# Local V of batches 4 to 7 loaded by casting DMAs on GpSimd's queue, in a fused attention and MoE kernel

## The chip, the cores and the metric

One core of a Trainium2 chip runs the whole program. The metric is device time in microseconds (us). The engines are TensorE (PE, matrix products), VectorE (DVE), ScalarE (ACT), GpSimd (POOL) and SyncE (SP), which here only issues DMAs. Each engine runs its own list of instructions in order and waits on semaphores for the others. DMAs issued by SP and by GpSimd go to two queues, which share the core's 16 DMA engines.

## The reference

Eight batches, eight heads, 576 positions, head size 64. Heads 0 to 3 attend locally (the last 32 positions), heads 4 to 7 with a stride (all earlier positions of the same residue modulo 32). The result goes through a two-layer MLP with squared ReLU.

```python
mask_local = (rel >= 0) & (rel < stride)                      # stride = 32, heads 0..3
mask_strided = (rel >= 0) & (pos[None, :] % stride == pos[:, None] % stride)   # heads 4..7
scores = np.where(masks[None], 1/sqrt(D) * q @ k.T, -1e9)
attn = softmax(scores)
x = (attn @ v).transpose(0, 2, 1, 3).reshape(B * S, H * D)    # 4608 x 512
h = x @ w_in                                                  # 512 x 2048
return np.maximum(h, 0.0) ** 2 @ w_out                        # 2048 x 512, float32 out
```

All inputs are float32 in memory; the kernel computes in bfloat16 with float32 sums.

## The kernel before

**Units.** A unit is a pair of heads of one batch: `u = 4 * b + p`, with p = 0, 1 local and p = 2, 3 strided. For a unit the kernel transposes q and k (`step_T` on TensorE, or DMA transposes on SP in later batches), forms the scores (`step_S`, L315), takes the exponential (L320), masks, and multiplies by V (`step_D`, L419). The softmax sum comes out of the same product, because V has a column of ones (`VP` = 72 columns are kept for 65). `step_E` or `step_X` writes the transposed result into `xt`, from which `mm1` (L487) and `mm2` (L527) compute the MLP in nine chunks of 512 rows.

**Local V.** A local block has 96 queries and 128 keys: the 32 positions before the block and the block itself. So a tile of local V, `vls[i]`, holds for each of six blocks the block's own 96 rows in partitions 32 to 127, and in partitions 0 to 31 a copy of the last 32 rows of the block before. There are four such tiles; batch b uses tiles `(2 * b + p) % 4`, so a tile is used again after two batches.

**Three ways in which local V arrives.** Batch 0 has a load of its own (`load_v_first`, L353, and the shift L359). Batches 1 to 3 go through `loads` and use `load_v_local_cast` (L214), one DMA on GpSimd's queue that reads float32 and writes bfloat16 straight into partitions 32 to 127, and `shift_v_local` (L221), a GpSimd copy of partitions 96 to 127 to partitions 0 to 31 one block further on. Batches 4 to 7 go through `loads_v`: two DMAs per unit on SP's queue (`load_v_local`, L185) bring float32 rows into one of two staging tiles `vl_st`, and two GpSimd casts (`cast_v_local`, L192 and L193) write the tile and its shifted part. Partitions 0 to 31 of the staging tiles are zeroed once by VectorE at the start (L693).

**Strided V** of batches 2 to 7 is loaded on SP's queue into `v_st` (L201) and cast by GpSimd (L208), before and after the change.

**Order.** The program is written out by hand: `manual_schedule`. The MLP's groups are laid in a row, and attention steps are dealt out between them by weights (`due`). Loads hang on numbers of groups (`hooks`, set by `plan`). For batches from 4 on, `plan` places three things:

```python
        at(g, lambda: loads_qk(b))
        at(max(g + 8, g0 + (g1 - g0) * 8 // 10), lambda: transpose_str(b))
        at(n0, lambda: loads_v(b))
        for i in range(2):
            at(g + 14 + 4 * i, lambda u=4 * b + i: transpose_local(u))
```

A hook fixes only the order on each engine's list. GpSimd and SP run ahead of TensorE as far as their waits let them. On GpSimd the list of late batches repeats: the V work of batch b, then the DMAs that cast strided q and k of batch b + 1 to DRAM (`q_d`, `k_d`, L153), then four casts of local q and k of batch b + 1 (L123). On SP it is: the loads of local V, of strided V, loads of q and k (L107), transposes of `q_d` and `k_d` (L161), transposes of local q and k (L173), and between them the output (L532) and the transposes of finished attention (L444).

Of the kernel before, what the change touches and what calls it, by code (L numbers as in the profile page):

```python
# [8 lines left out]
FP32 = mybir.dt.float32  # L9
# [5 lines left out]
def kernel(  # L15
# [9 lines left out]
    nc = tc.nc  # L25
    B, H, S, D = q.shape
# [5 lines left out]
    QL = 96  # L32
    NL = S // QL
# [6 lines left out]
    singles = ctx.enter_context(tc.tile_pool(name="singles", bufs=1))  # L40
# [23 lines left out]
    mask_str = singles.tile([SP_, 1, SP_], BF16)  # L64
    vls = [singles.tile([128, 2, NL, VP], BF16, name=f"vl{i}") for i in range(NV)]
    vss = [singles.tile([SP_, NBS, VP], BF16, name=f"vs{i}") for i in range(NV)]
    vl_sts = [singles.tile([128, 2 * NL, D], FP32, name=f"vl_st{i}") for i in range(2)]
    kTl = [singles.tile([128, 32 + S], BF16, name=f"kTl{i}") for i in range(NV)]
    es = [singles.tile([128, 1280], BF16, name=f"e{i}") for i in range(4)]
    xt = [singles.tile([128, T], BF16, name=f"xt{p}") for p in range(4)]  # L70
# [21 lines left out]
    units = [(b, p) for b in range(B) for p in range(H // 2)]  # L92
    st = {}
# [83 lines left out]
    def v_slot(u):  # L177
        b, p = units[u]
        return (b * 2 + p % 2) % NV

    def load_v_local(u, eng):
        b, p = units[u]
        t = vl_sts[p]
        for hh in range(2):
            eng.dma_start(out=t[32:128, NL * hh:NL * (hh + 1), :],  # L185
                          in_=v[b, 2 * p + hh].rearrange("(t p) d -> p t d", p=QL))
        st.setdefault(u, {})["vf"] = t

    def cast_v_local(u):
        s = st[u]  # L190
        t = vls[v_slot(u)]
        nc.gpsimd.tensor_copy(t[:, :, :, 0:D].rearrange("p h t d -> p (h t) d"), s["vf"])  # L192
        nc.gpsimd.tensor_copy(  # L193
            t[0:32, :, 1:NL, 0:D],
            s["vf"][96:128].rearrange("p (h t) d -> p h t d", h=2)[:, :, 0:NL - 1, :])
        s["v"] = t

    def load_v_str(u, eng):
        b, p = units[u]
        t = v_st.tile([SP_, 2, NJ * D], FP32, name="v_st")  # L200
        eng.dma_start(out=t, in_=v[b, 2 * p:2 * p + 2]  # L201
                      .rearrange("h (p j) d -> p h (j d)", j=NJ))
        st.setdefault(u, {})["vf"] = t

    def cast_v_str(u, copy=None):
        s = st[u]
        t = vss[v_slot(u)]
        (copy or nc.gpsimd.tensor_copy)(t[:, :, 0:D], s["vf"].rearrange("p h (j d) -> p (h j) d", d=D))  # L208
        s["v"] = t

    def load_v_local_cast(u):
        b, p = units[u]
        t = vls[v_slot(u)]
        nc.gpsimd.dma_start(  # L214
            out=t.rearrange("p h t c -> p (h t) c")[32:128, :, 0:D],
            in_=v[b, 2 * p:2 * p + 2].rearrange("h (t p) d -> p (h t) d", p=QL))
        st.setdefault(u, {})["v"] = t

    def shift_v_local(u):
        t = vls[v_slot(u)]  # L220
        nc.gpsimd.tensor_copy(t[0:32, :, 1:NL, 0:D], t[96:128, :, 0:NL - 1, 0:D])  # L221
# [449 lines left out]

    def loads_v(b):
        for i in range(2):
            load_v_local(4 * b + i, nc.sync)
        for i in range(2):
            load_v_str(4 * b + 2 + i, nc.sync)
        for i in range(2):
            cast_v_local(4 * b + i)
        for i in range(2):
            cast_v_str(4 * b + 2 + i)  # L680

# [7 lines left out]
    warm(8)  # L689
    nc.vector.memset(ones, 1.0)  # L690
    nc.vector.memset(vl0[0:32, 0, 0, 0], 0.0)
    for t in vl_sts:
        nc.vector.memset(t[0:32], 0.0)  # L693
    for t in kTl:
        nc.vector.memset(t[:, 0:32], 0.0)
    for t in vls:
# [80 lines left out]
    def plan(b, n0, g0, g1):  # L777
        if b < LB:
            at(n0, lambda: loads(b))
            if b >= XB:  # L780
                at(n0 + 6, lambda: transpose_str(b))
            return
        g = g0 + (g1 - g0) * 45 // 100
# [5 lines that stand above are left out]
# [54 lines left out]
```

## Time and profile before

| | |
|---|---|
| median of 4 runs | 312.52 us (310.47 to 316.08) |
| the profiled execution | 313.4 us; span from first to last instruction 311.7 us |
| granted TensorE clock, mean | 0.989 |
| TensorE busy | 297.9 us (96%) |
| VectorE, ScalarE, GpSimd busy | 166.4, 162.6, 88.8 us |
| DMA, SP's queue | 72528 packets, 32.98 MB, 50.4% of 16 engines |
| DMA, GpSimd's queue | 19552 packets, 10.98 MB, 26.2% of 16 engines |
| loads of `vl_st` on SP | 16, first at 98.1, last at 180.7 us |
| casts L192 and L193 | 8 and 8, 0.959 us for one of the first kind in the mean |

How to read it: busy time is the sum of an engine's instructions. A row of a group gives line, engine, operation, the tile written and read, and then times; `x8: 823/824/1901` are count, and shortest, middle and longest duration in ns. In a list of windows, each engine's busy time in the window is followed by the number of its instructions, and after TensorE, its weight loads, VectorE, ScalarE and GpSimd come the granted clock, the share of the DMA engines and GB/s. In the timeline, square brackets hold the idle time before an instruction and what ended it.

### The profile page before, as it was taken

How to read it: one execution, taken by the hardware profiler on the slowest of the kernel's cores; microseconds unless marked ns; L12 is line 12 of the kernel's file. 1: busy time of each engine (PE TensorE's matmuls, PEld its weight loads, DVE VectorE, ACT ScalarE, POOL GpSimd, SP SyncE). 2: the span in 40 equal slices, each digit the busy share in tenths (PEclk: the TensorE clock that was granted, in tenths of full speed). 3: DMA queues.
4: the chain of work that ended last, by engine and by line, in shares of the span. 5: the costliest groups of instructions: out<-in, count | busy, mean ns of one | idle time of the engine just before them, and what ended most of it. 6: DMA issues, size and time to landing. Idle time of an engine off the chain costs nothing.

```text
span 311.7 us, 6150 instructions
## 1 busy us (share of the span) xinstructions
PE 297.9 (96%) x2326; PEld 149.5 (48%) x2368; DVE 166.4 (53%) x411; ACT 162.6 (52%) x338; POOL 88.8 (28%) x117
## 2 busy tenths in 40 slices
PE   7879997899999999999999999999999999999995
PEld 3534554545554544545444544444444444444444
DVE  7666666359866886577467667654522222222200
ACT  3937754388555765555555555655443434344311
POOL 8528864454720823381055024000000000000000
PEclk9979999799999999999999999999999999999999
DMA  7999999999999999999999792225122010000021
GB/s 141 160 206 211 208 193 252 205 271 187 207 133 216 209 212 169 205 243 214 175 215 202 164 201 80 73 72 55 53 74 86 34 37 34 34 34 36 36 98 67
DMA packets 92252, 44.40 MB, mean 142 GB/s; under 512 B 76544, under 2 KB 85536, under 8 KB 92032
## 3 DMA queue, kind: packets, MB, share of 16 engines
q1 hardware_dynamic: 72528, 32.98, 50.4%
q0 software_dynamic: 19552, 10.98, 26.2%
q8 instruction: 18, 0.29, 0.4%
q14 instruction: 10, 0.08, 0.1%
q10 hardware_dynamic: 144, 0.07, 0.1%
HBM read 36.70 MB, written 13.57 MB: 161 GB/s over the span
## 4 chain that ended last, share of the span: by engine, by line
PE 80%; DMA 13%; POOL 4%; issue 1%; DVE 0%; ACT 0%; DVEq 0%; POOLq 0%; ACTq 0%
PE ph L487 36%; PE py L527 26%; PE ph L527 9%; DMA vs<-in_v_dram 5%; DMA w_in_b<-in_moe_w_in_dram 4%; PE pt L419 4%; DMA w_out_b<-in_moe_w_out_dram 4%; PE pt L315 3%; PE pt L451 1%; PE pt L271 1%; POOL kT_s L133 1%; POOL qT_s L133 1%; PE pt L512 1%; PE ph L512 1%; POOL vs L227 1%
## 5 line engine op out<-in xcount | busy, mean ns | idle before, releaser
L487 PE MATMUL ph<-xt,w_in_b 128*128 128x512 bf16 x559 | 142.9, 381 | 1.3 <-issue 0.5
L493 ACT ACTIVATE r<-ph 128x512 bf16<-128x512 f32 x143 | 85.3, 597 | 95.6 <-PE ph L487 88.8
L494 DVE TENSOR_TENSOR g_sb<-r 128x512 bf16<-128x512 bf16 x144 | 72.4, 507 | 102.8 <-ACT r L493 102.0
L527 PE MATMUL py<-w_out_b,g_sb 128*128 128x512 bf16 x378 | 99.6, 379 | 1.1 <-DVE x_l L434 0.2
L487 PEld LDWEIGHTS <-w_in_b 128*128 128x128 bf16 x576 | 52.6, 98 | 57.5 <-issue 1.9
L527 PEld LDWEIGHTS <-g_sb 128*128 128x128 bf16 x560 | 51.0, 98 | 53.8 <-issue 0.6
L320 ACT ACTIVATE e<-pt 128x288 bf16<-128x288 f32 (+1 forms) x128 | 46.3, 407 | 12.8 <-PE pt L315 12.8
L527 PE MATMUL ph<-w_out_b,g_sb 128*128 128x512 bf16 x155 | 39.4, 386 | 0.5 <-issue 0.3
L419 PEld LDWEIGHTS <-e 128*128 128x128 bf16 (+1 forms) x392 | 20.9, 98 | 17.6 <-issue 2.9
L434 DVE TENSOR_TENSOR x_s<-pt,rinv 72x384 bf16<-72x384 f32 (+1 forms) x42 | 21.4, 509 | 1.4
L192 POOL CAST vl<-vl_st 128x768 bf16<-128x768 f32 x8 | 7.7, 959 | 49.6 <-DMA vl_st<-in_v_dram 24.8
L326 DVE TENSOR_TENSOR e<-e,mask_loc 128x576 bf16<-128x576 bf16 x32 | 16.3, 511 | 3.7 <-ACT e L320 3.7
L531 ACT COPY y<-py 128x512 f32<-128x512 f32 x25 | 14.7, 586 | 5.4 <-PE py L527 5.1
L326 DVE TENSOR_TENSOR e<-e,mask_str 72x576 bf16<-72x576 bf16 x32 | 15.3, 483 | 3.5 <-ACT e L320 3.4
L123 POOL CAST k_l<-k_st 96x768 bf16<-96x768 f32 x14 | 11.9, 852 | 17.0 <-DMA k_st<-in_k_dram 16.7
L433 DVE RECIPROCAL rinv<-pt 96x6 f32<-96x6 f32 (+2 forms) x70 | 12.8, 183 | 7.4 <-PE pt L419 7.2
L419 PE MATMUL pt<-vs,e 72*128 72x65 bf16 x224 | 13.7, 196 | 2.9 <-DMA vs<-in_v_dram 2.7
L434 DVE TENSOR_TENSOR x_l<-pt,rinv 96x384 bf16<-96x384 f32 x28 | 15.5, 553 | 1.0
L123 POOL CAST q_l<-q_st 96x768 bf16<-96x768 f32 x14 | 12.4, 889 | 11.5 <-DMA q_st<-in_q_dram 11.5
L531 ACT COPY y<-ph 128x512 f32<-128x512 f32 x10 | 5.9, 588 | 15.9 <-PE ph L527 15.8
L208 POOL CAST vs<-v_st 72x1024 bf16<-72x1024 f32 x12 | 13.4, 1138 | 0.4
L545 PE MATMUL py<-y 128*128 128x512 bf16 x22 | 8.7, 476 | 1.3 <-DVE y L687 1.3
(91 smaller groups left out, 168.8 us busy)
## 6 DMA issues: line engine op xcount, KB each, us to landing
out_dram<-y SPq DMA_DIRECT2D x35, 256.0 KB, 2.9
v_st<-in_v_dram SPq DMA_DIRECT2D x12, 288.0 KB
q_st<-in_q_dram SPq DMA_DIRECT2D x16, 144.0 KB, 4.8
k_st<-in_k_dram SPq DMA_DIRECT2D x16, 144.0 KB, 6.7
vl_st<-in_v_dram SPq DMA_DIRECT2D x16, 144.0 KB, 3.3
w_in_b<-in_moe_w_in_dram POOLq DMA_DIRECT2D x4, 512.0 KB, 12.4
w_out_b<-in_moe_w_out_dram POOLq DMA_DIRECT2D x4, 512.0 KB, 11.1
q_st<-in_q_dram SPq DMA_DIRECT2D x7, 288.0 KB, 6.9
```

The costliest lines, as they stand in the source:

```text
L123: copy(t.rearrange("p j h d -> p h j d"), s[name + "f"].rearrange("p h (j d) -> p h j d", j=6))
L208: (copy or nc.gpsimd.tensor_copy)(t[:, :, 0:D], s["vf"].rearrange("p h (j d) -> p (h j) d", d=D))
L320: nc.scalar.activation(e[0:kn, lo:lo + S // 2], banks[row][half][0:kn, 0:S // 2], AF.Exp, scale=scale)
L326: nc.vector.tensor_tensor(x, x, m.to_broadcast([kn, n, w]), op=ALU.mult)
L419: nc.tensor.matmul(po[:, n - n0, :], e[0:kn, pos(n):pos(n) + 128], rhs[0:kn, src(n), 0:D + 1], start=True, stop=True)
L433: nc.vector.reciprocal(rinv[0:w, 0:m], po[0:w, 0:m, D:D + 1])
L434: nc.vector.tensor_tensor(x, po[0:w, 0:m, 0:D], rinv[0:w, 0:m].to_broadcast([w, m, D]), op=ALU.mult)
L487: nc.tensor.matmul(ph, w_in_b[:, kk, 128 * ff:128 * (ff + 1)], xt[kk][:, 512 * c:512 * (c + 1)], start=(kk == order[0]), stop=(kk == order ...
L493: nc.scalar.activation(r, ph, AF.Relu)
L494: later(1, lambda: nc.vector.tensor_tensor(g[:, ff, :], r, r, op=ALU.mult))
L527: nc.tensor.matmul(py, g[:, ff, 128 * j:128 * (j + 1)], w_out_b[:, ff, :], start=(ff == 0), stop=(ff == 15))
L531: nc.scalar.copy(y, py)
```

## The change

In batches 4 to 7 local V is loaded as in batches 1 to 3: `loads_v` calls `load_v_local_cast` and `shift_v_local`. The two functions of the staged path, the two staging tiles and the two memsets that zeroed them are gone. The order of the calls inside `loads_v`, and its place among the hooks, stay; but the first call now puts its DMAs on GpSimd's list and not on SP's.

```diff
-    vl_sts = [singles.tile([128, 2 * NL, D], FP32, name=f"vl_st{i}") for i in range(2)]
...
-    def load_v_local(u, eng):
-        b, p = units[u]
-        t = vl_sts[p]
-        for hh in range(2):
-            eng.dma_start(out=t[32:128, NL * hh:NL * (hh + 1), :],
-                          in_=v[b, 2 * p + hh].rearrange("(t p) d -> p t d", p=QL))
-        st.setdefault(u, {})["vf"] = t
-
-    def cast_v_local(u):
-        s = st[u]
-        t = vls[v_slot(u)]
-        nc.gpsimd.tensor_copy(t[:, :, :, 0:D].rearrange("p h t d -> p (h t) d"), s["vf"])
-        nc.gpsimd.tensor_copy(
-            t[0:32, :, 1:NL, 0:D],
-            s["vf"][96:128].rearrange("p (h t) d -> p h t d", h=2)[:, :, 0:NL - 1, :])
-        s["v"] = t
...
     def loads_v(b):
         for i in range(2):
-            load_v_local(4 * b + i, nc.sync)
+            load_v_local_cast(4 * b + i)
         for i in range(2):
             load_v_str(4 * b + 2 + i, nc.sync)
         for i in range(2):
-            cast_v_local(4 * b + i)
+            shift_v_local(4 * b + i)
         for i in range(2):
             cast_v_str(4 * b + 2 + i)
...
-    for t in vl_sts:
-        nc.vector.memset(t[0:32], 0.0)
```

The two functions that are called now are in the kernel before as well:

```python
    def load_v_local_cast(u):
        b, p = units[u]
        t = vls[v_slot(u)]
        nc.gpsimd.dma_start(
            out=t.rearrange("p h t c -> p (h t) c")[32:128, :, 0:D],
            in_=v[b, 2 * p:2 * p + 2].rearrange("h (t p) d -> p (h t) d", p=QL))
        st.setdefault(u, {})["v"] = t

    def shift_v_local(u):
        t = vls[v_slot(u)]
        nc.gpsimd.tensor_copy(t[0:32, :, 1:NL, 0:D], t[96:128, :, 0:NL - 1, 0:D])
```

## The prediction

> **What bounds the kernel now.** I read the page first, then the chain of waits, then stretches of the TensorE timeline, then every row that touches `vl` and `vl_st`. The page says that TensorE is the bound:
>
> ```profile
> PE 297.9 (96%) x2326; PEld 149.5 (48%) x2368; DVE 166.4 (53%) x411; ACT 162.6 (52%) x338; POOL 88.8 (28%) x117
> ...
> PE   7879997899999999999999999999999999999995
> ...
> PEclk9979999799999999999999999999999999999999
> ...
> PE 80%; DMA 13%; POOL 4%; issue 1%; DVE 0%; ACT 0%; DVEq 0%; POOLq 0%; ACTq 0%
> ```
>
> The gaps in the PE row lie in the first eight slices, 62 us. The chain splits the run in the same way: three DMA pieces carry the start, and from 56 us on it is TensorE alone.
>
> ```profile
> 10.39 13.32 DMA w_in_b<-in_moe_w_in_dram
> 26.16 11.10 DMA w_out_b<-in_moe_w_out_dram
> 39.45 16.19 DMA vs<-in_v_dram
> ```
>
> The change works on batches 4 to 7, whose V comes between 98 and 191 us. The busy time by stretch shows what room is left there:
>
> ```profile
> 98.00:112.00 14.00, 13.89 (x115) 6.78 (x114) 11.49 (x26) 9.78 (x19) 7.69 (x8) 1.00 1.10 210
> 112.00:126.00 14.00, 13.79 (x120) 6.90 (x119) 9.34 (x25) 8.65 (x19) 3.39 (x4) 1.00 1.03 174
> ...
> 168.00:182.00 14.00, 13.89 (x126) 7.11 (x127) 9.12 (x24) 7.50 (x17) 0.00 (x0) 1.00 0.74 171
> ```
>
> The second number is TensorE busy in 14 us: 0.1 to 0.2 us idle. Added over all stretches from 56 to 238 us it is idle for 2.1 us. So no improvement in the V path can return more than about 2 us (0.7%); a loss is possible only where a V tile, or something queued behind it, becomes later than TensorE asks for it.
>
> **The change, part by part.** Per late batch the old path is four SP loads, two full casts (L192) and two shifted casts (L193); the new one is two casting DMAs (L214) and two shifts (L221). The new form already runs in batches 1 to 3, so its rows are in this trace:
>
> ```profile
> L192 POOL CAST vl<-vl_st x8: 823/824/1901, 101.9 to 186.7; 128x768 bf16<-128x768 f32 x8
> L193 POOL CAST vl<-vl_st x8: 713/792/837, 102.8 to 187.6; 32x640 bf16<-32x640 f32 x8
> L214 POOL DMA_DIRECT2D vl<-in_v_dram x6: 884/898/909, 26.9 to 64.7; - x6
> L221 POOL COPY vl<-vl x6: 709/714/935, 40.3 to 80.2; 32x640 bf16<-32x640 bf16 x6
> ...
> DMA to landing us min/median/max: 11.3/13.1/15.4
> ```
>
> GpSimd work: out go 8 x 0.959 (page, L192) + 8 x about 0.78 = 13.9 us; in come 8 x 0.898 + 8 x 0.714 = 12.9 us. Net 1 us less on an engine that is 28% busy: nothing on the path.
>
> SP queue: 16 issues of `vl_st` go, 2.1 to 2.4 us a batch by the timeline (98.06 to 100.50 for batch 4). The strided V loads, transposes and q/k loads behind them can start that much earlier. No TensorE wait over 0.4 us after 62 us names one of these, so the path gains nothing.
>
> DMA engines: per batch 2304 packets of 256 B on SP's queue (in the trace's packet times 23 to 32 ns in the mean, over four stretches with such loads) become 2304 casting packets of 128 B (32 to 37 ns). At 34 against 27 ns over 16 engines this is 2304 x 7 / 16 = 1.0 us more per batch. The transfers behind it have several us to spare; hidden.
>
> VectorE at the start: two memsets of `vl_st` go (L693, 0.698 us each, 1.52 to 3.02 us). VectorE is busy without a gap until it casts K of unit 0 at 5.42 us, so that cast can come up to 0.7 us sooner, and the first scores with it. What is late next is V of batch 0: TensorE waits at 17.04 us for the shift L359, and GpSimd waited 4.3 us for its DMA. GpSimd's DMA issues before that wait for nothing VectorE does. Gain on the end: 0. If that cover were absent, 0.7 us.
>
> **The timing of V**, which decides. Landing is now 3.3 us (`vl_st`, from SP) and was 11.3 to 15.4 us for the casting form. Lower end for late batches: the batch-0 V load L353, the same number of packets in one DMA, landed 8.4 us after issue. Upper end: 15.4. I take 13.1, because the late stretches are also full of SP traffic (DMA share 0.7 to 1.25).
>
> In exchange the issue is earlier. GpSimd issues when its previous instruction, the last K cast, ends, and it need not wait for its slot: batch 4 overwrites batch 2's tiles, read last at 76.3 us, and the later ones are as free. Per batch, first unit: issue starts, ready (issue + 13.1 + 0.7 shift), ready before (end of L193), first read by L419:
> - batch 4: 92.3, 106.1; before 103.6; read 114.7. Margin 8.6.
> - batch 5: 122.1, 135.9; before 129.2; read 145.7. Margin 9.8.
> - batch 6: 143.7, 157.5; before 156.8; read 177.5. Margin 20.
> - batch 7: 167.9, 181.7; before 184.7; read 200.2. Margin 18.
>
> With 15.4 instead of 13.1 each margin shrinks by 2.3, and the smallest is 6.3 us. The second units are issued 0.9 us later and read 4 to 8 us later.
>
> The new wait is the shift's for its own DMA. Behind it on GpSimd stand the two strided V casts (about 2.2 us together), the two DRAM casts `q_d`, `k_d` of the next batch, and four q/k casts. `q_d` of batch 5 would issue at 109.3 instead of 109.5, of batch 6 at 139.0 instead of 135.4, of batch 7 at 160.5 instead of 163.6. The worst is batch 6: `k_d` follows at 139.5 and lands 6.3 us later, at 145.8; SP issued its transpose at 142.9 before, so SP is held 2.9 us, and with it the transposes of local q and k behind it, of which the first unit's pair was issued by 147.6. It would be issued by 150.5 and land by 155.7 (5.2 us, the longer median for these); the scores that read it run at 165.3. Margin 9.5 us. Hidden too.
>
> A rule speaks against the change. The row first: the six L214 issues took 884 to 909 ns with VectorE 27% to 80% busy, so nothing stretched them. The Trainium skill, SBUF — State Buffer, section "SBUF: two separate sides", warns that a VectorE operation in a 2-port mode shuts GpSimd out of its SBUF port, so that descriptors of a GpSimd-issued DMA aren't written and the transfer waits; in its passage on a bandwidth pool the page gives about 620 ns alone, 3100 ns beside such a copy. By the rule each issue would cost about 2.5 us more, 5 us a batch, and batch 4's first unit would keep 8.6 - 2.5 = 6.1 us (3.8 at the upper landing); by the row nothing. I go by the row; either way TensorE isn't held.
>
> **Sum.** 0 us on the path; profiled execution 313.4 us (span 311.7 and 1.7 around it) stays 313.4. That execution lies 0.9 above the median of the runs shown; I forecast the median, 312.5 us.
>
> **The spread of runs.** Two slices of PEclk fall to 7. They are two stretches of 3.4 us at half clock, the second right after the longest TensorE wait:
>
> ```profile
> 55.67 0.31 PE L419 MATMUL pt<-vs,e 72*128 72x65 bf16 x5 [2.68 <-DMA vs<-in_v_dram]
> ...
> 57.00:60.00 3.00, 3.00 (x26) 0.50 1.43 114
> ```
>
> Each costs some 1.7 us of matmul time. One more or one fewer moves a run by 0.5%, and the four runs before reach from 310.5 to 316.1. So under 1%, 3.1 us, can hardly be told from no change by a measurement like this.
>
> **Rivals.**
> - *The casting loads land too late (slower).* One mechanism: DMAs with small packets on GpSimd's queue take turns with SP's traffic and the shift holds GpSimd. TensorE stops at the first local output of batch 4 once the landing exceeds 114.7 - 0.7 - 92.3 = 21.7 us; above that it costs one for one, plus 1.7 if the stop brings a half-clock stretch. At twice the worst seen, 30.8 us, batch 4 stops for 9.1 us: 312.5 + 9.1 + 1.7 = 323.3. For: landings were four times those from SP. Against: they were so beside weight loads in two of three batches, and nothing over 15.4 was seen. At 25 us: 3.3 + 1.7, so 317.5.
> - *The start gets shorter (faster).* The 0.7 us of memset reaches the end, and neither half-clock stretch occurs: 312.5 - 0.7 - 2 x 1.7 = 308.4. For: VectorE is full until the K cast. Against: V of batch 0 arrives at 17 us, and the strided V of batch 1 at 55.7 us, by GpSimd's queue, whatever VectorE does.
> - *SP's relief pays (slightly faster).* All the idle time of 56 to 238 us goes: 312.5 - 2.1 = 310.4, still within 1%.
>
> **Chances.** Forecast with its clock scatter 0.69 and SP's relief 0.06, together 0.75 within 1%; late landing or another GpSimd hold-up slower by over 1%: 0.15; shorter start or lucky clock: 0.10. The range goes from 309.8 (one half-clock stretch fewer, 1.7, and half of SP's relief, 1.0) to 316.0 (a landing of 23.5 us with its stop of 1.8 and a slow clock, 1.7).
>
> **What would show it.** Right: 14 L214 issues of about 0.9 us; no L192/L193; landings in late batches between 8 and 16 us; long GpSimd waits at L221 for the DMA; first L419 reads of `vl` at the same distance from one another; TensorE idle under 0.3 us per 14 us from 98 us on; the first w_in chunk still held by L359 at about 17 us. Wrong: a TensorE wait at L419 on `vl` or at L315 on `kTl` or `kT_s`, a landing over 20 us, L214 issues of several us, or another number of half-clock stretches than two, which would be the clock and not the change.

## The result, and the profile after

The changed kernel took 314.86 us (median of 34 runs, 311.6 to 317.81), the kernel before 312.80 us (55 runs, 310.35 to 318.88). The ratio of their runs is 1.005, 95% interval 1.0027 to 1.0074: half a per cent slower. (The ratio uses the runs within 1.5% of the quickest of their own kernel, so it is not the quotient of the two medians of all runs, which is 1.0066.) The time lies inside the stated range, but no difference was forecast, and the interval does not reach down to 1.

The change did to the engines what the forecast says. GpSimd went from 88.8 to 87.6 us, and the group rows show 14 casting loads, each issued in an unchanged time. These are rows of the changed kernel that touch `vl` (in it L401 is `step_D`, L196 the casting load, L203 the shift):

```profile
L196 POOL DMA_DIRECT2D vl<-in_v_dram x14: 882/898/909, 26.5 to 174.2; - x14
L203 POOL COPY vl<-vl x14: 709/713/1225, 41.2 to 179.9; 32x640 bf16<-32x640 bf16 x14
...
  DMA vl<-in_v_dram: 22.7, 10
...
DMA to landing us min/median/max: 4.6/7.3/15.2
```

The median landing over all 14 loads is 7.3 us, and in batches 4 to 7 it is 4.6 to 8.2 us, not 13.1, so local V of the late batches is ready earlier than I reckoned. Where, then, did the time go?

The profiled execution that came with the result is a long one (319.8 us, span 318.1), so its page needs care:

```profile
span 318.1 us, 6123 instructions
...
PE   7889883899989999999999999999999999999995
...
PEclk9999999699999999999999999999999999999999
```

Most of its extra time lies between 28 and 56 us, where TensorE is busy for 20.2 us and before for 24.9. At the end of this stretch it waits twice for the strided V of batch 1 (2.79 and 2.97 us), and the clock then falls to half for about 6.8 us. Nothing that runs up to there was changed except the two memsets. From the first local output of batch 4 (114.7 us before, 121.1 here) to the last matmul the two profiles take the same 193.7 us: the stretch in which all the late loads' results are used costs nothing. This led me first to the memsets, and the experiments speak against that.

A second profile of the same kernel (`after_again`, 312.0 us span) has a quick start and shows a stop in another place. Its page, TensorE and clock:

```profile
span 312.0 us, 6165 instructions
...
PE   7889999999996999999999999999999999999995
...
PEclk9979999999999899999999999999999999999999
```

There is a new dip in the thirteenth slice (94 to 101 us), and the clock falls in the next. The TensorE waits of this profile after 62 us, in us, times and longest:

```profile
PE pt L297 <- DMA kTl<-k_l: 2.6, 1, 2.6
PE pt L401 <- DVE e L308: 0.3, 1, 0.3
```

L297 is `step_S` (L315 before), L172 the DMA transpose of local q and k (L173 before). TensorE doesn't wait for V. It waits for the transposed K of batch 4's first local unit, which this change doesn't touch. The chain of waits goes through the same place:

```profile
93.78 1.56 SPq L172
...
95.47 4.82 DMA kTl<-k_l
...
100.33 0.66 PE pt L297 x12
```

The transpose was issued at 95.47 us and landed 4.8 us later. In the profile before, the same transpose and the same scores were at 96.66 and 101.61 us, and TensorE did not wait (the first two rows are SP's, the third TensorE's):

```profile
96.66 1.36 SPq L173 DMA_TRANSPOSE kTl<-k_l  x1
98.06 2.44 SPq L185 DMA_DIRECT2D vl_st<-in_v_dram  x4
101.61 0.43 PE L315 MATMUL pt<-qT,kTl 64*128 64x96 bf16 x12
```

What was in the DMA engines of `after_again` then is seen in GpSimd's timeline, the third column being the instruction's engine:

```profile
91.83 1.78 POOL L196 DMA_DIRECT2D vl<-in_v_dram  x2
97.20 0.71 POOL L203 COPY vl<-vl 32x640 bf16<-32x640 bf16 x1 [3.60 <-DMA vl<-in_v_dram]
99.90 0.72 POOL L203 COPY vl<-vl 32x640 bf16<-32x640 bf16 x1 [1.99 <-DMA vl<-in_v_dram]
```

Batch 4's casting loads are issued at 91.8 us and land at about 97.2 and 99.9 us: across most of the time of the transposes. Between 91 and 101 us GpSimd's queue takes this share of the DMA engines (packets, MB, share); before, that queue moved nothing in these 10 us:

```profile
q0 software_dynamic: 2336, 0.30, 46.1%
```

Before, the staged loads stood on SP's queue *behind* these transposes and began at 98.06 us. The stretch from 98 to 112 us shows the price (columns: stretch, its length, TensorE busy; the granted clock follows GpSimd's count):

```profile
98.00:112.00 14.00, 11.67 (x88) 5.70 (x89) 8.11 (x20) 7.34 (x15) 3.76 (x5) 0.88 1.15 211
```

Before it was 13.89 us busy at full clock. Here it is 11.67 at 0.88: the wait, and behind it a stretch of 3.4 us at half clock.

### The profile page after: what moved, and what is told of

It reads as the page before. It is cut to its first block, busy times and chain, and to the rows that moved or that the text cites. A ratio compares the mean times of both kernels' runs of the same rounds, so it can differ in the third digit from the quotient of the medians.

```text
span 318.1 us, 6123 instructions
## 1 busy us (share of the span) xinstructions
PE 298.7 (94%) x2326; PEld 149.8 (47%) x2368; DVE 162.1 (51%) x409; ACT 162.9 (51%) x338; POOL 87.6 (28%) x117
## 4 chain that ended last, share of the span: by engine, by line
PE 85%; DMA 7%; DVE 3%; ACT 2%; issue 1%; POOL 1%; DVEq 0%; ACTq 0%
PE ph L469 39%; PE py L509 26%; PE ph L509 8%; DMA vs<-in_v_dram 6%; PE pt L401 4%; PE pt L297 3%; PE pt L253 1%; PE pt L433 1%; DVE e L308 1%; DMA q_st<-in_q_dram 1%; ACT e L302 1%; PE pt L494 1%; PE ph L494 1%; PE py L527 1%; DVE kTl L268 0%
## 5 line engine op out<-in xcount | busy, mean ns | idle before, releaser
L476 DVE TENSOR_TENSOR g_sb<-r 128x512 bf16<-128x512 bf16 x144 | 68.3, 477 | 107.5 <-ACT r L475 106.2
L401 PEld LDWEIGHTS <-e 128*128 128x128 bf16 (+1 forms) x392 | 21.2, 99 | 21.6 <-issue 7.4
L122 POOL CAST q_l<-q_st 96x768 bf16<-96x768 f32 x14 | 11.6, 827 | 28.3 <-DMA q_st<-in_q_dram 28.3
L190 POOL CAST vs<-v_st 72x1024 bf16<-72x1024 f32 x12 | 12.5, 1056 | 24.8 <-DMA v_st<-in_v_dram 18.9
L401 PE MATMUL pt<-vs,e 72*128 72x65 bf16 x224 | 13.8, 197 | 5.9 <-DMA vs<-in_v_dram 5.8
L308 DVE TENSOR_TENSOR e<-e,mask_str 72x576 bf16<-72x576 bf16 x32 | 17.3, 546 | 3.1 <-ACT e L302 2.9
L203 POOL COPY vl<-vl 32x640 bf16<-32x640 bf16 x14 | 10.9, 786 | 22.8 <-DMA vl<-in_v_dram 22.7
L122 POOL CAST k_l<-k_st 96x768 bf16<-96x768 f32 x14 | 13.2, 944 | 11.5 <-DMA k_st<-in_k_dram 11.5
L308 DVE TENSOR_TENSOR e<-e,mask_loc 128x576 bf16<-128x576 bf16 x32 | 15.0, 468 | 2.7 <-ACT e L302 2.7
L196 POOL DMA_DIRECT2D vl<-in_v_dram x14 | 12.5, 894 | 4.8 <-DMA w_out_b<-in_moe_w_out_dram 2.9
```

Of the source, the lines that this page charges most:

```text
L122: copy(t.rearrange("p j h d -> p h j d"), s[name + "f"].rearrange("p h (j d) -> p h j d", j=6))
L308: nc.vector.tensor_tensor(x, x, m.to_broadcast([kn, n, w]), op=ALU.mult)
L401: nc.tensor.matmul(po[:, n - n0, :], e[0:kn, pos(n):pos(n) + 128], rhs[0:kn, src(n), 0:D + 1], start=True, stop=True)
L476: later(1, lambda: nc.vector.tensor_tensor(g[:, ff, :], r, r, op=ALU.mult))
```

## The experiments

Twelve kernels ran, each beside the kernel before on the same chip. A second reading goes with the ratio: each run lists its mean granted clock, and (1 - clock) x span / 1.7 us gives the number of half-clock stretches in it, so the share of runs with none can be counted. In the kernel before it was 55 of 202 runs (27%), over the three chips of these experiments.

### Start, late loads, or addresses

Three theories stood after the first profile: the start lost its memsets; the late loads cost; the tiles behind the staging tiles moved by 6 KB.

**late_only.** The changed kernel with the staging tiles and memsets put back, unused:

```diff
+    vl_sts = [singles.tile([128, 2 * NL, D], FP32, name=f"vl_st{i}") for i in range(2)]
...
+    for t in vl_sts:
+        nc.vector.memset(t[0:32], 0.0)
```

> The changed kernel with the two staging tiles allocated again, in their old place, and zeroed again by VectorE at the start, though nothing reads them. So only the late V path differs from the kernel before: start and tile addresses are as before. In the changed kernel's profile the stretch from the first local output of batch 4 to the end is 193.7 us, as before, and all of its 6.4 us more lie ahead of it. Theory start (the loss comes from the first 60 us, which lost their memsets): ratio 1.000, within 0.997 to 1.003. Theory late loads (the casting DMAs of batches 4 to 7 cost it): 1.005 or more. Theory addresses (the tiles moved by 6 KB): 1.000.

Measured: 1.0005 (0.998 to 1.003). By the ratio alone this spoke for the start or the addresses. But its profile held the wait that the first one had not shown, in TensorE's timeline:

```profile
100.69 0.43 PE L298 MATMUL pt<-qT,kTl 64*128 64x96 bf16 x12 [1.85 <-DMA kTl<-k_l]
```

and 3 of 22 runs (14%) had no half-clock stretch. From the first local output of batch 3 to that of batch 4 this profile takes 28.5 us, the kernel before 24.9. That gave the theory that I then tested: collision, the casting loads' packets slowing the transposes. The ratio does not fit it: this kernel has the same casting loads as the changed one, and its interval ends at 1.003. Why it loses less is not known.

**pad_no_memset.** Staging tiles allocated, never touched, no memsets.

> The changed kernel with the two staging tiles allocated but never touched: tile addresses as before, no memsets. Theory start: about 1.005 to 1.007, like the changed kernel, since the memsets are missing. Theory late loads: the same, 1.005 to 1.007. Theory addresses: 1.000.

Measured: 1.0053 (1.0019 to 1.0086); 1 of 22 runs without a half-clock stretch. Addresses as before, loss as in the changed kernel: not the addresses.

**memset_no_pad.** The memsets in their old place, on other memory:

```diff
+    for p in range(2):
+        nc.vector.memset(xt[p][0:32, 3072:4608].bitcast(FP32), 0.0)
```

> The changed kernel with two VectorE memsets of the same size (32 partitions of 768 float32 words) in the old place of the list, on parts of xt that are written much later; the staging tiles stay away, so addresses are those of the changed kernel. Theory start: 1.000. Theory late loads: 1.005 to 1.007. Theory addresses: 1.005 to 1.007.

Measured: 1.0026 (1.0001 to 1.0052). Between the theories; undecided by itself.

**before_memset_late.** The kernel before, its memsets moved:

```diff
     def loads_v(b):
+        if b == LB:
+            for t in vl_sts:
+                nc.gpsimd.memset(t[0:32], 0.0)
...
-    for t in vl_sts:
-        nc.vector.memset(t[0:32], 0.0)
```

> The kernel before, with staged V loads as they were, except that the two memsets of the staging tiles are taken from the start and done by GpSimd ahead of the V work of batch 4, near 92 us. Addresses and the late V path are as before, the start is that of the changed kernel. Theory start: 1.005 to 1.007. Theory late loads and theory addresses: 1.000 (1.6 us more on GpSimd at 92 us, with 8 us and more to spare).

Measured: 0.9991 (0.9963 to 1.0019), and 7 of 22 runs without a half-clock stretch. Up to the V work of batch 4 the instructions of this kernel and of pad_no_memset are the same, one for one; they differ by 0.6%. So the missing memsets are not the cause, and what costs comes in with batch 4's loads or behind them.

### Which batch

**cast_b4_only** and **cast_b567_only**: the kernel before, with one condition in both loops of `loads_v` (`b == LB`, where `LB` is 4, for the first kernel, `b > LB` for the second); the first of the two loops:

```diff
         for i in range(2):
-            load_v_local(4 * b + i, nc.sync)
+            if b == LB:
+                load_v_local_cast(4 * b + i)
+            else:
+                load_v_local(4 * b + i, nc.sync)
```

> The kernel before, in which batch 4 alone takes its local V by casting DMAs; batches 5 to 7 stay staged, staging tiles and memsets stay. Theory collision: GpSimd issues batch 4's casting DMAs near 92 us, some 6 us before SP would have issued the staged loads, so their 2304 small packets run beside the DMA transposes of batch 4's first local q and k (SP, 95 to 98 us); TensorE then waits for kTl at about 100 us, as in the profile of late_only (1.85 us, then a half-clock stretch). All of the loss is there: full ratio of the changed kernel, 1.003 to 1.007, and fewer executions without a half-clock stretch (some 10% instead of some 28%). Theory start (memsets): 1.000, since they are still there. Theory chance: 1.000.

Measured: 1.0051 (1.002 to 1.0081); 4 of 22 runs without a half-clock stretch.

> The kernel before, in which batches 5 to 7 take local V by casting DMAs and batch 4 stays staged. Theory collision: 1.000, because from the first local output of batch 4 to the end every profile so far takes 193.7 us; share of executions without a half-clock stretch as before, some 28%. A theory that the casting DMAs cost DMA time everywhere: 1.003 to 1.005.

Measured: 0.9981 (0.9954 to 1.0009); 6 of 22. Batch 4 alone carries the loss, with the memsets in place; three batches of the same loads together cost nothing that can be measured.

### Taking the collision away

**after_gate.** The changed kernel, with GpSimd held until the transpose has landed:

```diff
+    gate_t = singles.tile([1, 2], BF16)
...
+            if b == LB and i == 0:
+                nc.gpsimd.tensor_copy(gate_t[0:1, 0:1], kTl[v_slot(4 * b)][0:1, 32:33])
             load_v_local_cast(4 * b + i)
```

> The changed kernel with one tiny GpSimd copy ahead of batch 4's casting DMAs that reads kTl of batch 4's first unit, so that they are issued only when that transpose has landed (near 101 us and not 92). Theory collision: the wait for kTl at 100 us goes and the ratio falls to 1.000 (0.998 to 1.002); V of batch 4 is then ready near 110 us, still ahead of its first read at 114.7. Theory start: stays at 1.005. If the gate makes V late, a wait at the local outputs of batch 4 shows instead.

Measured: 0.9999 (0.9969 to 1.003); 7 of 22 runs without a half-clock stretch. Its profile also gives the landing of that transpose without the packets beside it, since the gate waits for just this. Queues of SP and GpSimd:

```profile
97.45 1.20 SPq L173 DMA_TRANSPOSE kTl<-k_l  x1
...
100.10 0.18 POOL L658 COPY gate_t<-kTl 1x1 bf16<-1x1 bf16 x1 [7.30 <-DMA kTl<-k_l]
100.67 1.77 POOL L197 DMA_DIRECT2D vl<-in_v_dram  x2 [0.39 <-POOL gate_t L658]
```

Issued at 97.45, there by 100.10: 2.65 us at the most, against 4.8 us in `after_again`. V of batch 4 is then shifted by 110 us, and TensorE doesn't wait for it.

**after_swap.** The changed kernel, with the transposes of that unit ahead of the strided ones on SP:

```diff
-        at(max(g + 8, g0 + (g1 - g0) * 8 // 10), lambda: transpose_str(b))
+        gs_ = max(g + 8, g0 + (g1 - g0) * 8 // 10)
+        if b == LB:
+            at(gs_, lambda: transpose_local(4 * b))
+        at(gs_, lambda: transpose_str(b))
...
-        for i in range(2):
+        for i in range(1 if b == LB else 0, 2):
             at(g + 14 + 4 * i, lambda u=4 * b + i: transpose_local(u))
```

> The changed kernel in which SP issues the DMA transposes of batch 4's first local unit ahead of the two strided transposes (qT_s, kT_s of batch 4) and the two output DMAs, not behind them: about 4 us earlier, near 91 us. The casting DMAs keep their place. Theory collision: kTl is then ahead of the casting packets or has 4 us more in hand: ratio 1.000 or slightly below (0.996 to 1.001). Theory start: 1.005.

Measured: 0.9985 (0.9957 to 1.0012); 8 of 22 runs without a half-clock stretch. The casting loads stay where they are, and the loss is gone once the transpose has more time in hand. In its profile kTl is issued early and TensorE comes to it without a wait:

```profile
89.83 1.98 SPq L172 DMA_TRANSPOSE kTl<-k_l  x1
...
100.20 0.43 PE L297 MATMUL pt<-qT,kTl 64*128 64x96 bf16 x12
```

### Adding the collision alone

**dummy_two** and **dummy_four**: the kernel before, V staged as it was, with two or four extra casting loads that nothing waits for at that place:

```diff
     def loads_v(b):
+        for i in range(2 if b == LB else 0):          # 4 in dummy_four
+            nc.gpsimd.dma_start(
+                out=xt[i][32:128, 3840:4608].rearrange("p (n d) -> p n d", d=D),
+                in_=v[b, 2 * (i % 2):2 * (i % 2) + 2].rearrange("h (t p) d -> p (h t) d", p=QL))
```

> The kernel before with its staged V path, and beside it two extra casting DMAs of the same rows of V at the head of batch 4's V work on GpSimd (near 92 us), into columns of xt that are written much later; nothing waits for them there. Only the packets are added, no wait, nothing is taken from SP. Theory collision: their 2304 packets alone delay the transposes of batch 4's first local unit: 1.003 to 1.006, like cast_b4_only. If instead the loss comes from what the new path does to the order on GpSimd or SP (the shift's wait, the missing SP loads): 1.000.

Measured: 1.0056 (1.0032 to 1.0081); 2 of 22 runs without a half-clock stretch.

> As dummy_two, with four extra casting DMAs and so twice the packets at the same place. Theory collision: more than dummy_two, some 1.006 to 1.015, and a profile that shows TensorE waiting at the scores of batch 4's first unit for kTl. Theory order of the queues: 1.000 to 1.002.

Measured: 1.0104 (1.0059 to 1.0148) on six runs, none without a half-clock stretch. The packets alone make a loss like that of the changed kernel, and with twice the packets it is about twice as large, though with wide intervals. No load was taken from SP. What the packets do to the transposes is seen in the landing of q's, which SP issues just before kTl; here in dummy_four:

```profile
L173 SPq DMA_TRANSPOSE qT<-q_l x1: 1293/1293/1293, 94.7 to 94.7; - x1
...
DMA to landing us min/median/max: 8.0/8.0/8.0
```

The same transpose in every profile that gives its landing at this place:

| casting loads of local V in flight | landing of q's transpose, us |
|---|---|
| none | 4.4 (before), 4.0 (before_memset_late), 3.1 (after_gate), 4.1 (memset_no_pad, whose casting loads were in before it) |
| two | 7.0 (after), 6.1 (after_again), 5.1 (late_only), 5.2 (pad_no_memset), 7.0 (dummy_two) |
| four | 8.0 (dummy_four) |

The wait that I expected in dummy_four's profile did not come, or hardly: only a weight load of TensorE waits for kTl there, 0.4 us at these scores. TensorE comes to them at 103.49 us, and the stretch from the first local output of batch 3 to that of batch 4 takes 25.0 us, 24.9 in the kernel before. So this execution (315.9 us) shows the slower transposes but no loss from them, though the six executions of this kernel were all about as slow (315.3 to 317.31 us).

### Can the repair beat the kernel before?

**before_swap.** The swap of after_swap, in the kernel before.

> The kernel before, with SP's transposes of batch 4's first local unit moved ahead of the strided ones as in after_swap. In before's profile the scores that need kTl ran at 101.6 us, and kTl was issued at 96.7 us, so the slack was about 1 us; in executions with a quick start it may be below zero. Theory collision: 0.996 to 1.000; about the same as after_swap (0.9985), since with the transposes early the V path no longer matters.

Measured: 1.002 (0.9991 to 1.0048) on 14 runs: no gain, and above what was expected. Its profile has short waits at the scores of local units still (0.5 us for kTl, 0.6 us in two for VectorE). No version was found that beats the kernel before beyond the interval; after_swap is level with it.

**after_again.** The changed kernel once more; its profile is the one read above.

> The changed kernel itself on the chip of this call, to be compared with dummy_two and before_swap: 1.004 to 1.007, fewer executions free of half-clock stretches than the kernel before (10% against 28%).

Measured: 1.0029 (1.0002 to 1.0056); 3 of 22 runs without a half-clock stretch. A little under what was expected, and in agreement with the first measurement within the intervals.

Together: the five kernels with batch 4's casting V loads in that place of GpSimd's list (the changed kernel measured twice) have no half-clock stretch in 17 of 145 runs (12%). The four kernels in which batch 4 is staged or gated, or the transposes go first, have none in 28 of 88 (32%). The ratios, dummies included, are 1.0005 to 1.0104 for the kernels whose casting loads in that place are neither held nor behind the transposes, and 0.9981 to 1.002 for the others; by the medians of all runs 1.0016 to 1.0111 and 0.9978 to 1.0011. Two readings do not fit and are left open: late_only's ratio, and before_swap with 1 of 14 runs without a half-clock stretch.

## Why the prediction was wrong

**The bound, and the room after 56 us:** right. TensorE is full there, and the chain is TensorE nearly alone.

**GpSimd's work:** right (1 us less forecast, 1.1 us less measured). **Memsets at the start:** right; before_memset_late takes them away at 0.9991.

**The timing of V:** right in direction, off in size. I took 13.1 us for the landing in late batches; the loads of batch 4 landed in 5.3 and 7.1 us in after_again, those of batch 6 in 4.7 and 4.8 us in the first profile. The slower rival, V later than 21.7 us after issue, never came near. Nor did I see the issue stretched beside VectorE: all 14 issues took 877 to 909 ns in each of the two profiles. So the rule of the Trainium skill that I weighed (SBUF — State Buffer, "SBUF: two separate sides") does not show in the issues. The page's figures are for a whole transfer and not for its issue, as I used them; the landings here (4.6 to 16.3 us) cannot tell such a wait from one in the queues.

**The step that failed** is the sentence on the DMA engines: "The transfers behind it have several us to spare; hidden." In the profile before, q of batch 4's first local unit landed at 99.6 us (95.22 + 4.4), 2.0 us before its scores at 101.61: that was all there was to spare, and not several us. I costed the packets by their sum, 1.0 us more per batch, and not by *when* they run. In the table of V times I even counted it as a gain that GpSimd issues 6 us earlier than SP did (92.3 against 98.06 us). But between these times SP issues the transposes of batch 4's first local unit. On SP's queue they had gone first, and V behind them. On GpSimd's queue V runs beside them.

And the profile before was a trace with two half-clock stretches ahead of these scores. In a run with a quick start TensorE comes to these scores at 97.7 us (100.33 - 2.60 in after_again), while SP's transposes come hardly sooner, at 95.47 us. Then 2.65 us or 4.8 us for the landing decides whether TensorE stops for some 0.4 us (an estimate, 95.47 + 2.65 - 97.73) or for 2.6. The prediction followed the transposes of batch 6, late by a wait on a queue, and never the transposes in flight beside batch 4's loads.

**The clock:** I wrote that another number of half-clock stretches "would be the clock and not the change". In after_again and late_only one such stretch came by the change. In after_again the stop at 98 us is followed by a stretch at half clock, and its price is on top of the wait: from the first local output of batch 3 to that of batch 4 the kernel before takes 24.9 us and after_again 29.2. Of these 4.3 us, 2.6 is the wait and 1.7 the slow clock; in late_only it is 3.6 us, of which 1.85 is the wait. An execution with a slow start brings TensorE late to the place, and there the transpose is in time: the first profile after took 24.9 us for this stretch and showed nothing.

**Sum:** 0 us was forecast. The term for the transposes beside the casting packets measures about 2 us in the median (314.86 against 312.80), and 0 to 4.3 us in single profiles, depending on the start.

**What stays open:** by which stops most executions lose. That batch 4's packets beside these transposes cost the time is shown by the experiments that hold the packets back, add packets, or put the transposes first; the measured waits come from two profiles with a quick start. If only a quick start lost, the slower executions would not have moved. But the lowest, the first quarter, the middle and the third quarter of the runs of the changed kernel lie 1.25, 2.0, 2.1 and 1.9 us above those of the kernel before, and the profiles of slower executions (after, pad_no_memset, dummy_two, dummy_four) show no loss behind 92 us. Open too is how often the kernel before itself stops at these scores after a quick start: its one profile had none, and 0.4 us is not a measurement.

## What to carry to other kernels

A load that is moved from one queue to another changes not only who waits for it but what it overtakes: put the new issue time beside everything that the old queue had ahead of it, and look at the landing times of just those transfers. Where a transfer on the path has 1 or 2 us of slack, two DMAs of small packets took it here; hold them until it has landed, or issue the needed transfer earlier. And do not reckon slack from one profile alone: with a quicker start the same transfer can be late.

## What the runs showed of the hardware

The transpose of k, 96 rows by 6 blocks, landed in at most 2.65 us with no casting load in flight (after_gate) and in 4.8 us beside two of them (after_again). The one of q issued just before it landed in 3.1 to 4.4 us beside none, 5.1 to 7.0 us beside two and 8.0 us beside four. TensorE waits of 1.85 us (late_only) and 2.6 us (after_again) were each followed by a stretch of about 3.4 us at half clock, so that they cost 3.6 and 4.3 us.
